# Moving the sums of weights to one engine, and earlier starts for raw weights and first-stage steps, in a fused Fourier-mixing and feed-forward kernel

## The chip, the cores and the metric

The kernel runs on one core of one Trainium2 chip. The metric is the device time of one execution in microseconds (us), as the median of several runs. The core has five engines, each of which takes its own instructions in order: TensorE (PE, matrix products into PSUM), VectorE (DVE), ScalarE (ACT), GpSimd (POOL) and SyncE (SP, which here only issues transfers). Transfers between HBM and SBUF are issued from SP, ACT and POOL and run on 16 DMA engines. Semaphores tie the engines together.

## The reference

```python
def _attn_ref(x, filt_r, filt_i):            # x: 8 x 3008 x 256
    X = np.fft.rfft(x, axis=1)
    F = (filt_r + 1j * filt_i)[None, :, :]   # 1505 x 256
    return np.fft.irfft(X * F, n=x.shape[1], axis=1)

def _moe_ref(x, w_in, w_out):                # x: 24064 x 256, w_in: 256 x 2048, w_out: 2048 x 256
    h = x @ w_in
    g = h - np.tanh(h)
    return g @ w_out
```

The second function works on the result of the first. The two weight matrices arrive as 64-bit floats, which the kernel reads as pairs of 32-bit words.

## The kernel before

**Stages.** The length of 3008 is 64 x 47. A sequence is transformed in stages of matrix products: a first stage (`first`, L273; `first0` and `first1` for the first two sequences), a middle (`middle`) that finishes the transform, multiplies by the filter and goes back half of the way, and a last stage (`last`, L526) that gives a group of 4 x 128 positions in transposed form. Between the stages the data goes through HBM (`ct1`, `ct2`). The feed-forward part then runs on each group.

**Units.** One group has four units, U = 4i + u, and a unit is one quarter u of the hidden width. In loop step U of the main loop (L1284) TensorE makes the first product of unit U (`up`, L565, or `up_plain`, L637, for U under 4), ScalarE and VectorE the activation of unit U - 1 (`shrink`, L678), and TensorE the second product of unit U - 2 (`down`, L729, or `down_plain`). `up` and `down` use seven products where eight would be needed, on sums of the weights: `wu` and `wd` have seven slots each, of which four are loaded and three (slots 4, 5 and 2) are sums; slot 6 is overwritten as well. `up_plain` and `down_plain` use the four loaded slots alone, so group 0 can run before the sums are there. The sums of quarter u of `wu` are `sums(u)`, those of `wd` are `sums(4 + u)`: one addition and three subtractions of 128x256 (L220 to L228). The activations need their own combinations for the seven products: `combine` (L557), of 128x512 for `t` and of 128x256 for `tu`, on GpSimd once all weights are ready.

**Raw weights.** `converted` (L165) loads 128x512 raw values (512 KB) and makes 32-bit floats of them: one ScalarE instruction (L175), then five or six of VectorE (L177 to L195). `weights` (L237) is a generator over 16 such jobs, of which jobs 5 to 15 run beside the start of the main loop, on buffers lent by the middle stage (`ft`, `a2`, `xy`), loaded from GpSimd's queue. After certain jobs it goes on with sums (`after`, L1208).

**The order.** All instructions stand in the order in which the Python program emits them; there is no scheduler. Inside a unit `up` calls back: `d` and `e` advance the second product, `s` the activation, `t(k)`, k = 0 to 4, everything else. `converting(n)` (L1310) takes n instructions from the generator `late` (the weights, and from U = 6 on a list of sums): two in each `t`, three in each of four `e`. `t(k)` at position 20c + 5u + k of a sequence (c is the group in it) also takes one step of one other stage: `last` at (u, k) = (3, 2), otherwise a step of the first stage of sequences 1 and 2 when the next entry of `due` (L1278) has come, in units 0 to 3 at any k and later only at k = 2.

**A first-stage step** here is `x_sb` and `f` loaded two steps ahead from SP, eight matmuls (L295) into the two PSUM banks with the tags t and y, two ScalarE copies (L297) into the single buffer `a1`, and a write to HBM from ScalarE's queue (L300). `last` uses the banks t and y too (`pu`, L537; copies at L541, L544, L545); `up` accumulates in banks x, y and z, each held once, and VectorE empties them at L601 (y), L618 and L634 (z) and L626 (x).

**Before the loop.** Sequence 0 goes through all stages first. Its last transfers are e2, the reload of `ct2` for the first `last` (`rest`, L1034). GpSimd then copies one column of e2 to `there_yet` (L1203), so that its next instructions, the raw loads of jobs 7 and 8 (L169), wait for e2. TensorE runs products that nobody reads (`warmer`, L999) until the first `pu`.

Of the kernel before, what the change touches and what calls it, by code (L numbers as in the profile page):

```python
# [9 lines left out]
F32 = mybir.dt.float32  # L10
# [17 lines left out]
NX = NH // XH  # L28
# [10 lines left out]
LEAD = 34  # L39
# [72 lines left out]
def kernel(  # L112
# [10 lines left out]
    V, G, ACT = nc.vector, nc.gpsimd, nc.scalar  # L123
# [14 lines left out]
    cst = ctx.enter_context(tc.tile_pool(name="cst", bufs=1))  # L138
# [81 lines left out]
    def sums(u):  # L220

        w = (wu if u < 4 else wd)[:, :, 256 * (u % 4):256 * (u % 4) + 256]
        by = G if 4 <= u < 7 else V
        by.tensor_add(w[:, 4], w[:, 6], w[:, 3])
        yield
        for to, one_in, less in ((5, 4, 0), (2, 1, 5), (6, 0, 6)):
            by.tensor_sub(w[:, to], w[:, one_in], w[:, less])
            yield  # L228

    def begun(tiles, job, queue=nc.sync):  # L230
# [6 lines left out]
    def weights(tiles, jobs, queue, began, ahead, after=()):  # L237

        began += [begun(tiles, job, queue) for job in jobs[len(began):ahead]]
        yield  # L240
        for k in range(len(jobs)):
            pending[0] = len(jobs) - k
            for n, _ in enumerate(began[k]):
                yield
                if after and n == 2 and k + 1 < len(jobs):
                    next(began[k + 1])
            if k + ahead < len(jobs):
                began.append(begun(tiles, jobs[k + ahead], queue))
            pending[0] = len(jobs) - k - 1
            for u in dict(after).get(k, ()):  # L250
                yield from sums(u)
# [272 lines left out]
    e2s, uts = {}, {}  # L524
# [38 lines left out]
    hs, gs = {}, {}  # L563

    def up(U, d, e, s, t):  # L565

        i, u = divmod(U, 4)
# [32 lines left out]
        shrinks(0)  # L600
        V.tensor_add(h[:, 0, :, 0:w], Y, s1)  # L601
        e()
        shrinks(1)
        if not close:
# [7 lines left out]
        d()  # L612
        shrinks(3)
        e()
        t(2)
        mm(X, 7, False)
# [333 lines left out]
    with tc.tile_pool(name="tr", bufs=2) as tr, tc.manual_schedule():  # L950
# [16 lines left out]
        with tc.tile_pool(name="pro", bufs=1) as pro, \  # L967
# [66 lines left out]
            def rest(a, n, queues):  # L1034

                e2 = e2s[0][0]
                for j in range(4):
                    queues[j % len(queues)].dma_start(
                        e2[NA * j + a:NA * j + a + n],
                        dram(ct2[0], (NA * j + a) * NH * DM, [[NH * DM, n], [1, CH * DM]]))  # L1040
# [128 lines left out]
            for g in range(last_g + 1):  # L1169
# [27 lines left out]
                if g == 2:  # L1197
# [1 line left out]
            rest(0, SG * (last_g - 1), [nc.sync])  # L1199
            way_back()  # L1200
            rest(SG * (last_g - 1), NA - SG * (last_g - 1), [nc.sync])
            there_yet = cst.tile([128, 1], F32, name="there_yet")
            G.tensor_copy(there_yet, e2s[0][0][:, 0, 0:1])  # L1203
            fs = first(2, z2, [(1, c) for c in range(2, NX)])
            next(fs)
            convert(100)
            late = weights(tiles1, jobs[5:], G, ahead, 3,
                           after={6: (0,), 8: (1,), 10: (2, 3, 4, 5, 6)})  # L1208
            next(late)
            for _ in ones_1:  # L1210
                pass
# [2 lines left out]
        with tc.tile_pool(name="dn", bufs=2) as dn, \  # L1214
# [60 lines left out]
                                 start=True, stop=True)  # L1275
            for _ in range(4):
                next(late)
            due = [7 + (LEAD - 7) * k / (NX + 4) for k in range(NX + 4)]  # L1278
            plan = []
            kinds = {(2, 0): "there", (1, 3): "back"}  # L1280
            kinds.update({at: "filter" for at in FILTERED})
# [2 lines left out]
            for U in range(total + 2):  # L1284
                i, u = divmod(U, 4)
                if U == 6:
                    assert not pending
                    late = sums(7)
                if U == 3:
                    G.dma_start(mats[:, 0:10 * PAD], wide_d[0:KM])  # L1290
                if U < total:
# [18 lines left out]
                def converting(n):  # L1310

                    for _ in range(n):
                        if next(late, pending) is pending:
                            pending.clear()
# [5 lines left out]
                def e():  # L1320

                    next(dw, None)
                    converting(3 if U > 1 else 1)

                def s():

# [85 lines left out]
```

## Time and profile before

| | us |
|---|---|
| median of 3 runs | 2584.98 |
| lowest and highest run | 2583.92, 2587.75 |
| the profiled execution | 2587.2 |
| its span, first to last instruction | 2585.3 |
| TensorE busy | 2556.4 |
| VectorE busy | 1821.1 |
| ScalarE busy | 1661.8 |
| GpSimd busy | 1475.9 |

The profile comes from one execution; its span is 1.9 us shorter than its time. A line of the view by order of time has the start in us from the span's start, the time taken, engine, line, operation, out<-in, shapes, the number of instructions merged, and in brackets the idle time of the engine just before and what ended it ("issue": nothing that the profile shows). A transfer's line is its issue and not its landing. PE rows are matmuls; PEld, the weight load, overlaps them.

### The profile page before, as it was taken

Reading aid. Unit: us, or ns where it says so; the run is one execution under the profiler, and the core shown is the slowest. Engines: PE = TensorE matmul, PEld = TensorE weight load, DVE = VectorE, ACT = ScalarE, POOL = GpSimd, SP = SyncE. Lnnn points to the kernel's source line nnn. Section 1 sums busy time; section 2 is a strip of 40 time slices with the busy share of each in tenths; the row PEclk is TensorE's granted clock in tenths of the full one; section 3 lists DMA queues with packets and bytes.
Section 4 is the critical chain, followed back from the end, with each engine's and each line's share of the span. In section 5 each row is a group of like instructions: output and inputs, shape, how many; then the busy total and the mean of one; then the engine's idle time right before and its main releaser. Section 6 shows DMA issues by size and latency. Waiting matters only on the chain.

```text
span 2585.3 us, 43442 instructions
## 1 busy us (share of the span) xinstructions
PE 2556.4 (99%) x16596; PEld 2176.2 (84%) x16596; DVE 1821.1 (70%) x2222; ACT 1661.8 (64%) x2482; POOL 1475.9 (57%) x1138
## 2 busy tenths in 40 slices
PE   8999999999999999999999999999999999999998
PEld 7668888888898888988888888888889888898887
DVE  6877776877567775778657876588766877555555
ACT  4556666666666666666666666666666666666665
POOL 5366665666556665665646565466655766545552
PEclk9999999999999999999999999999999999999999
DMA  8863216441434324333243432444231322110110
GB/s 222 265 178 105 70 30 123 111 102 44 95 75 106 86 59 93 84 88 94 50 101 80 102 78 51 94 96 103 66 71 42 93 66 43 33 32 18 25 21 18
DMA packets 345333, 214.30 MB, mean 83 GB/s; under 512 B 245337, under 2 KB 316535, under 8 KB 341469
## 3 DMA queue, kind: packets, MB, share of 16 engines
q1 hardware_dynamic: 321551, 170.82, 28.7%
q10 hardware_dynamic: 12142, 23.60, 3.0%
q0 software_dynamic: 11424, 17.03, 2.4%
q8 instruction: 132, 2.16, 0.3%
q14 instruction: 84, 0.69, 0.1%
HBM read 130.72 MB, written 83.39 MB: 83 GB/s over the span
## 4 chain that ended last, share of the span: by engine, by line
PE 96%; DVE 1%; DMA 1%; issue 0%; ACT 0%; POOL 0%; ACTq 0%; DVEq 0%; POOLq 0%
PE o L748 43%; PE x L578 25%; PE z L578 12%; PE y L578 6%; PE pm L360 2%; PE pu L537 2%; PE pf L307 1%; PE o L803 1%; PE pf L295 1%; PE o L648 0%; DMA fh<-f 0%; PE pm L362 0%; DMA neg<-in_filt_i_dram 0%; DMA mats_sb<-mats 0%; PE x L648 0%
## 5 line engine op out<-in xcount | busy, mean ns | idle before, releaser
L748 PE MATMUL o<-t,wd 128*128 128x256 f32 (+1 forms) x3008 | 762.1, 376 | 0.0
L558 POOL TENSOR_TENSOR t<-h 128x512 f32<-128x512 f32 (+1 forms) x186 | 305.3, 1641 | 740.1 <-DVE h L700 718.7
L700 DVE TENSOR_TENSOR h<-h,y 128x1024 f32<-128x1024 f32 (+1 forms) x384 | 577.3, 1503 | 165.4 <-ACT y L696 161.8
L748 PEld LDWEIGHTS o<-t,wd 128*128 128x128 f32 x3008 | 569.2, 190 | 82.4 <-POOL o L776 15.1
L578 PE MATMUL x<-tu,wu 128*128 128x256 f32 (+1 forms) x2256 | 579.0, 379 | 0.0
L748 PE MATMUL o<-h,wd 128*128 128x256 f32 (+1 forms) x2256 | 572.8, 376 | 1.8 <-DVE h L700 1.8
L584 ACT COPY s<-x 128x512 f32<-128x512 f32 (+1 forms) x188 | 108.8, 579 | 601.3 <-PE x L578 556.5
L748 PEld LDWEIGHTS o<-h,wd 128*128 128x128 f32 x2256 | 426.0, 190 | 71.4 <-issue 20.5
L578 PEld LDWEIGHTS x<-tu,wu 128*128 128x128 f32 x2256 | 420.9, 190 | 66.8 <-issue 13.5
L693 ACT ACTIVATE y<-y 128x1024 f32<-128x1024 f32 (+1 forms) x384 | 399.3, 1040 | 12.1
L696 ACT ACTIVATE y<-y 128x1024 f32<-128x1024 f32 (+1 forms) x384 | 399.8, 1041 | 4.6
L690 ACT ACTIVATE y<-h 128x1024 f32<-128x1024 f32 (+1 forms) x384 | 400.3, 1042 | 3.5 <-DVE h L626 1.7
L559 POOL TENSOR_TENSOR t<-h,t 128x512 f32<-128x512 f32 (+1 forms) x186 | 306.2, 1646 | 14.6
L560 POOL TENSOR_TENSOR t<-h 128x512 f32<-128x512 f32 (+1 forms) x186 | 288.4, 1551 | 0.0
L561 POOL TENSOR_TENSOR t<-h,t 128x512 f32<-128x512 f32 (+1 forms) x186 | 287.4, 1545 | 0.0
L584 ACT COPY u<-x 128x512 f32<-128x512 f32 (+1 forms) x376 | 213.7, 568 | 56.6 <-PE x L578 53.9
L626 DVE COPY h<-x 128x512 f32<-128x512 f32 (+1 forms) x188 | 127.9, 680 | 136.7 <-PE x L578 136.4
L578 PE MATMUL z<-ut,wu 128*128 128x256 f32 (+1 forms) x752 | 191.1, 377 | 3.6 <-DVE h L618 3.6
L578 PE MATMUL x<-ut,wu 128*128 128x256 f32 (+1 forms) x752 | 190.7, 376 | 0.0
L578 PE MATMUL y<-ut,wu 128*128 128x256 f32 (+1 forms) x752 | 190.0, 375 | 0.0
L578 PE MATMUL z<-tu,wu 128*128 128x256 f32 (+1 forms) x752 | 190.0, 375 | 0.0
L601 DVE TENSOR_TENSOR h<-y,s 128x512 f32<-128x512 f32 (+1 forms) x188 | 126.6, 673 | 69.6 <-PE y L578 62.3
(197 smaller groups left out, 2758.0 us busy)
## 6 DMA issues: line engine op xcount, KB each, us to landing
ft<-filt SPq DMA_DIRECT2D x28, 1024.0 KB
ct<-nn SPq DMA_DIRECT2D x56, 512.0 KB
e<-ct SPq DMA_DIRECT2D x47, 512.0 KB
a<-ct SPq DMA_DIRECT2D x112, 192.0 KB
out_dram<-ot SPq DMA_DIRECT2D x1248, 16.0 KB
x_sb<-in_x_dram SPq DMA_DIRECT2D x74, 256.0 KB
ct<-a ACTq DMA_DIRECT2D x62, 256.0 KB
gt<-g_pairs SPq DMA_DIRECT2D x42, 128.0 KB
```

What stands on the lines that cost most here:

```text
L558: by.tensor_sub(t[0], b[0][1], b[0][0])
L559: by.tensor_sub(t[1], b[1][1], t[0])
L560: by.tensor_sub(t[2], b[1][1], b[0][1])
L561: by.tensor_sub(t[3], b[1][0], t[1])
L578: nc.tensor.matmul(bank[:, k], wu[:, q - 1, (2 * u + k) * 128:(2 * u + k + 1) * 128], rhs[q - 1], start=(first and k == 0), stop=True, ski ...
L584: ACT.copy(t, X)
L626: V.tensor_copy(h[:, 2, :, 0:w], X)
L690: ACT.activation(y[k], ht[k], AF.Arctan, scale=TURN)
L693: ACT.activation(y[k], y[k], AF.Tanh, scale=BEND)
L696: ACT.activation(y[k], y[k], AF.Square, scale=SCALE, accum_out=y_sums[:, 2 * U + k // 2:2 * U + k // 2 + 1])
L700: V.tensor_mul(ht[k], ht[k], y[k])
L748: nc.tensor.matmul(product(q), wd[:, q - 1, (2 * u + k) * 128: (2 * u + k + 1) * 128], rhs[q - 1][:, k], start=(u == 0 and k == 0 and q == ...
```

## The change

Three things. All sums are made on VectorE; those of three quarters of `wd` were on GpSimd. Of the sums that followed the last raw weights (wu's quarters 2 and 3, wd's 0, 1 and 2), only wu's quarter 2 and wd's quarter 0 stay there; wu's quarter 3 and wd's 1, 2 and 3 are spread over units 6 and 7, two instructions in each `t` and none in `e`. The copy to `there_yet` is gone, so the raw loads behind it wait only for their own buffers. The dues of the first-stage steps of sequences 1 and 2 start at position 4 and not 7, with the same end.

```diff
     def sums(u):
         w = (wu if u < 4 else wd)[:, :, 256 * (u % 4):256 * (u % 4) + 256]
-        by = G if 4 <= u < 7 else V
-        by.tensor_add(w[:, 4], w[:, 6], w[:, 3])
+        V.tensor_add(w[:, 4], w[:, 6], w[:, 3])
         yield
         for to, one_in, less in ((5, 4, 0), (2, 1, 5), (6, 0, 6)):
-            by.tensor_sub(w[:, to], w[:, one_in], w[:, less])
+            V.tensor_sub(w[:, to], w[:, one_in], w[:, less])
             yield
...
-            there_yet = cst.tile([128, 1], F32, name="there_yet")
-            G.tensor_copy(there_yet, e2s[0][0][:, 0, 0:1])
...
             late = weights(tiles1, jobs[5:], G, ahead, 3,
-                           after={6: (0,), 8: (1,), 10: (2, 3, 4, 5, 6)})
+                           after={6: (0,), 8: (1,), 10: (2, 4)})
...
-            due = [7 + (LEAD - 7) * k / (NX + 4) for k in range(NX + 4)]
+            due = [4 + (LEAD - 4) * k / (NX + 4) for k in range(NX + 4)]
...
                 if U == 6:
                     assert not pending
-                    late = sums(7)
+                    late = (None for u in (3, 5, 6, 7) for _ in sums(u))
...
                     next(dw, None)
-                    converting(3 if U > 1 else 1)
+                    converting((U < 6) * (3 if U > 1 else 1))
```

LEAD is 34 and NX is 6, so there are ten steps.

## The prediction

> **What bounds the kernel now.** I read the page first, then the windows by stage, then the order of time of TensorE, VectorE, GpSimd and ScalarE where TensorE is not full. From the page:
>
> ```profile
> span 2585.3 us, 43442 instructions
> ...
> PE 2556.4 (99%) x16596; PEld 2176.2 (84%) x16596; DVE 1821.1 (70%) x2222; ACT 1661.8 (64%) x2482; POOL 1475.9 (57%) x1138
> ...
> PE 96%; DVE 1%; DMA 1%; issue 0%; ACT 0%; POOL 0%; ACTq 0%; DVEq 0%; POOLq 0%
> ```
>
> TensorE is busy 99% of the span, and the chain of work is 96% TensorE. Matmuls are neither added nor removed, so the change can only move TensorE's idle time (2585.3 - 2556.4 = 28.9 us) and the time in which its clock is held down. The windows say where both lie (columns: stretch, its length, then busy us of PE, PEld, DVE, ACT, POOL, granted clock, DMA share, GB/s):
>
> ```profile
> 128.00:136.00 8.00, 5.88 (x15) 3.71 (x15) 6.23 (x15) 3.51 (x7) 4.09 (x6) 0.79 0.85 224
> 136.00:156.00 20.00, 15.04 (x53) 9.97 (x52) 19.66 (x25) 8.51 (x14) 18.98 (x23) 0.98 0.76 213
> ```
>
> From 128 to 156 us TensorE stands for 7.1 us. That is units 3 and 4 (a unit is one quarter of the hidden width of one group), where the sums of weights are made. In the second stretch VectorE and GpSimd are both full. TensorE in order of time:
>
> ```profile
> 120.54 1.89 PE L295 MATMUL pf<-x_sb,f 128*128 128x256 f32 x8
> ...
> 130.35 3.00 PE L295 MATMUL pf<-x_sb,f 128*128 128x256 f32 x8 [2.12 <-issue]
> 133.14 2.37 PE L648 MATMUL o<-ut,wu 128*128 128x448 f32 x4
> 135.34 1.67 PE L803 MATMUL o<-h,wd 128*128 128x448 f32 x4
> 136.85 1.03 PE L578 MATMUL x<-ut,wu 128*128 128x256 f32 x4
> ...
> 145.73 1.13 PE L295 MATMUL pf<-x_sb,f 128*128 128x256 f32 x4 [1.40 <-DVE h L601]
> ...
> 155.16 2.08 PE L578 MATMUL z<-ut,wu 128*128 128x256 f32 x4 [3.57 <-DVE h L618]
> 157.03 1.73 PE L578 MATMUL x<-ut,wu 128*128 128x256 f32 x4
> ```
>
> Three waits: A 2.12, B 1.40, C 3.57 us. After A and C the next matmuls are slow: 3.00 against 1.89 and 2.37 against 1.67 (together 1.8 us), then 2.08 and 1.73 against 1.03 (1.75 us). After B only 0.1 is lost. With that A costs 3.9, B 1.5, C 5.3: 10.7 us.
>
> The Trainium skill, "TensorE: Matmul & The Clock Gate", section "What's actually happening", has the clock fall after about 3.4 us without work. Here 2.12 us was enough (clock 0.79 in the first window), so the row decides.
>
> **The change part by part.**
>
> *1. The step behind the `pu` matmuls (wait A).* First-stage matmuls write the PSUM banks t and y. The step at 130.35 stands next but one behind `pu`, which fills the same banks, and VectorE empties them only here:
>
> ```profile
> 129.57 0.68 DVE L545 TENSOR_TENSOR ut<-pu,odd 128x512 f32<-128x512 f32 x1
> ```
>
> It ends at 130.25, and the step starts. The new dues put steps at positions 4, 7, 10, 13, 16, 19 instead of 7, 10, 13, 16, 18, so the built order has one more step at the end of unit 0 and this one two products later, at the end of unit 3. The extra step (1.7 us) is taken out of unit 9, which nets to nothing. Between `pu` and the moved step now lie three products of 1.5 us; the banks are free in time and A's 3.9 us goes. What is late next: the step now stands right before unit 4, whose second product writes bank y. ScalarE must copy the step out first, and its one buffer a1 is free only when the previous step's write has landed:
>
> ```profile
> 125.28 0.33 ACTq L300 DMA_DIRECT2D ct<-a  x1
> ...
> 133.88 1.07 ACT L297 COPY a<-pf 128x512 f32<-128x512 f32 x2 [4.01 <-DMA ct<-a]
> ```
>
> That is 8.6 us from issue to copy. The previous step's copies stand about 1 us later in the new order (one step more ahead of them), so these end near 133.88 + 1.07 + 1.1 = 136.1. Unit 4 begins at 136.85 - 3.9 + 1.7 = 134.65, and y is wanted one product of 0.86 later, at 135.5. Price 0.6; bounds 0 (a write shorter by 0.6) and 4 (longer by 1.6, with the clock's 1.8).
>
> *2. The sums leave GpSimd (waits B and C).* Sums 4, 5, 6 were twelve instructions on GpSimd, of which these rows are the first and the last:
>
> ```profile
> 138.17 0.74 POOL L224 TENSOR_TENSOR wd<-wd 128x256 f32<-128x256 f32 x1
> ...
> 151.68 0.96 POOL L227 TENSOR_TENSOR wd<-wd 128x256 f32<-128x256 f32 x1 [0.57 <-PE o L803]
> ```
>
> VectorE alone (the first four rows) and beside them:
>
> ```profile
> 122.24 0.69 DVE L188 SCALAR_TENSOR_TENSOR xy<-a,xy 128x512 f32<-128x512 uint32 x1
> 122.97 0.76 DVE L195 TENSOR_TENSOR wd<-xy 128x256 f32<-128x256 f32 x2
> ...
> 125.75 1.08 DVE L700 TENSOR_TENSOR h<-h,y 128x896 f32<-128x896 f32 x1
> ...
> 132.09 0.42 DVE L224 TENSOR_TENSOR wu<-wu 128x256 f32<-128x256 f32 x1
> ...
> 138.31 0.89 DVE L186 TENSOR_SCALAR xy<-xy 128x512 int32<-128x512 int32 x1
> ...
> 140.37 2.97 DVE L195 TENSOR_TENSOR wd<-xy 128x256 f32<-128x256 f32 x2
> ...
> 147.17 1.62 DVE L188 SCALAR_TENSOR_TENSOR xy<-a,xy 128x512 f32<-128x512 uint32 x1
> 148.83 1.70 DVE L195 TENSOR_TENSOR wd<-xy 128x256 f32<-128x256 f32 x2
> 150.45 1.61 DVE L700 TENSOR_TENSOR h<-h,y 128x896 f32<-128x896 f32 x1
> 151.98 0.94 DVE L224 TENSOR_TENSOR wu<-wu 128x256 f32<-128x256 f32 x1
> ```
>
> The last five lose 2.21, 0.93, 0.94, 0.53 and 0.52 against the rows above them, 5.1 us; five smaller ones, of which the 0.89 is the first, bring it to 7.3. VectorE's order up to unit 6 hardly changes: where the four sums of wu's last quarter stood (behind L224 at 151.98) stand the four of wd's first. So L618, which ends C, comes up to 7.3 us earlier. TensorE wants it earlier too: by the 5.0 us of B and C, and by A less part 1's price, 3.9 - 0.6 = 3.3. 8.3 against 7.3 leaves 1.0, and L626 behind three sums (0.42 each) holds the next x for some 0.6. Price 1.6; bounds 0 and 3.8 (only the five quoted rows recovered). A gap below 1.4 costs no clock. Parts 1 and 2 save 10.7 - 0.6 - 1.6 = 8.5.
>
> *3. Sixteen sums in units 6 and 7.* Before, four stood there; now sums 3, 5, 6, 7 do: twelve more, 0.42 each. They stand in groups of two. The four of sums 5 fall into unit 6, where VectorE waits for others (1.17 before its L618, in the first of these rows):
>
> ```profile
> 183.46 0.69 DVE L618 TENSOR_TENSOR h<-z,u 128x512 f32<-128x512 f32 x1 [1.17 <-ACT u L584]
> ...
> 195.57 0.69 DVE L544 TENSOR_TENSOR ut<-pu,odd 128x512 f32<-128x512 f32 x1 [0.80 <-ACT odd L541]
> ...
> 196.78 0.68 DVE L618 TENSOR_TENSOR h<-z,u 128x512 f32<-128x512 f32 x1
> ```
>
> Sums 6 and 7 fall into unit 7, ahead of its L618, while GpSimd combines t and later tu:
>
> ```profile
> 171.27 1.27 POOL L558 TENSOR_TENSOR t<-h 128x512 f32<-128x512 f32 x1 [13.08 <-DVE h L700]
> ...
> 187.07 2.19 POOL L558 TENSOR_TENSOR t<-h 128x512 f32<-128x512 f32 x1 [6.56 <-DVE h L700]
> ...
> 193.65 2.25 POOL L561 TENSOR_TENSOR t<-h,t 128x512 f32<-128x512 f32 x1
> ```
>
> ```profile
> 199.19 1.03 PE L578 MATMUL z<-ut,wu 128*128 128x256 f32 x4
> ```
>
> L618 ends at 197.46 and TensorE wants it at 199.19: 1.7 us of slack, with 0.8 idle ahead of L544 it is 2.5. Eight sums cost 3.4 alone; beside GpSimd 0.85 each (half of the pair at 148.83), 6.8. So 0.9 to 4.3 us of wait; I take 2.0, nearer the low end, because GpSimd's four instructions end at 195.9 whatever stands beside them, and half of the sums come later. An upper bound is among the rivals.
>
> *4. Raw weights no longer wait for e2.* Before, GpSimd stood until e2's reload was in:
>
> ```profile
> 82.39 0.18 POOL L1203 COPY there_yet<-e 128x1 f32<-128x1 f32 x1 [12.74 <-DMA f<-f_both]
> 82.93 0.74 POOL L169 DMA_DIRECT2D a<-in_moe_w_out_dram  x1 [0.37 <-issue]
> ```
>
> ```profile
> 83.51 1.27 PE L537 MATMUL pu<-gt,e 64*64 64x64 f32 x64
> ```
>
> Now two loads of 512 KB start up to the 12.7 us earlier for which that instruction kept GpSimd waiting, beside e2's last write and reload. VectorE can't use them sooner: its first instruction on them stands behind L544 of the first `pu`. So there is no gain here but 1 MB less traffic right after, where the extra step's 1.3 MB comes in. The loss: e2 has 1.1 us of slack (82.39 to 83.51, covered by the warming matmuls). What queued loads do to such a write, with raw loads in flight and without:
>
> ```profile
> ct<-e POOLq DMA_DIRECT2D x2, 240.0 KB, 6.6
> ...
> ct<-e POOLq DMA_DIRECT2D x4, 240.0 KB, 3.1
> ```
>
> Bounds: nothing, and 3.5 on the write and 3.5 on the reload less 1.1, 5.9. Those two stood in GpSimd's own queue behind the raw loads; e2's go by SyncE and ScalarE. I take 1.0.
>
> **Sum.** 8.5 - 2.0 - 1.0 = 5.5 us off 2585.3 of span, so 2581.7 for that execution (2587.2). The median of the runs is 2585.0; from it, 2579.5.
>
> **Rivals.**
> *R1, all hidden.* Sums fit between PSUM copies and e2 keeps its slack: 2585.0 - 8.5 = 2576.5. For it: VectorE's waits of 1.17 and 0.80; against it: the 1.7 us at L618. The Trainium skill, "DMA: Bandwidth & Descriptors", section "Queues, rings and completion order", says that each DMA engine alternates between queues packet by packet, which would keep e2 from standing behind the raw loads; no row here shows raw loads in one queue slowing another.
> *R2, part of it is eaten.* Unit 7 waits over 2 us and pays the clock (2.0 + 1.8 more), or the write chain of a1 takes its bound (3 more): 2582 to 2584.
> *R3, slower: VectorE becomes the bound in unit 7.* If a sum beside GpSimd must wait for a whole instruction of it, the pair at 140.37 is the price (2.97 / 2 = 1.49 each): 8 x 1.49 - 2.5 + 1.8 = 11.2, so 2585.0 - 8.5 + 1.0 + 11.2 = 2588.7; at 2.19 each (t's row) 2594. It decides from about 1.2 us a sum. Against it: t's four instructions can hold VectorE only while they run. The Trainium skill, "SBUF - State Buffer", section "Who interferes with whom", has the port that the two engines share locked for a whole instruction, the loser blocked; L195's 2.97 agrees, but t's 2.19 against its 1.27 at 171.27 shows that the loss falls on both.
> *R4, nothing.* B and C are VectorE's own backlog and return behind wd's first sums: about 2585. Against it: the slow rows lie exactly where GpSimd adds.
>
> **How the numbers follow.** A measurement tells 0.2% (5.2 us) from no change. Forecast 0.45 (2576.8 to 2582), R1 0.15, R2 0.22, R3 0.12, R4 0.06. Faster by over 0.2% is below 2579.8: of the forecast's own 0.45 some 0.30, R1's 0.15, and 0.03 of cases with still less waiting, 0.48. Slower by over 0.2% is above 2590.2: R3's upper half and e2 at its bound, 0.10. The rest, 0.42. Range 2574.3 to 2588.7: from R1 with parts 1 and 2 free of their price (2585.0 - 10.7) to R3's lower price.
>
> **What would show it.** Part 1: no wait of L295 behind `pu`, y of unit 4 behind ScalarE's L297. Part 2: L195 at 0.76 a pair in unit 4, wait C under 1 us. Part 3: waits for L618 or L626 around unit 7. Part 4: `pu` later than 83.5. A `pu` later by over 3 us, or a wait over 6 us in unit 7, makes the forecast wrong; so does a TensorE clock that stays down after a short gap.

## The result and the profile after

| | before | after |
|---|---|---|
| median, us (12 runs each, taken together) | 2588.08 | 2582.41 |
| lowest and highest run, us | 2583.92, 2591.72 | 2580.93, 2585.17 |
| ratio of after to before, with its 95% interval | | 0.9979 [0.9971, 0.9986] |
| the profiled execution, us | 2587.2 | 2582.09 |
| its span, us | 2585.3 | 2580.2 |

The change saves 0.21%, 5.4 to 5.7 us. The prediction said 5.5 us; its 2579.5 stands below the 2582.4 measured because the three runs that it started from had a median 3.1 us below that of the twelve. All ratios here are of runs in the fast state; three of e9's seven runs (3816 to 6900 us) are in the slow one, so that its ratio rests on four.

In the changed kernel lines 224 to 1201 of before have numbers lower by one and those behind 1203 lower by three: L294 is the first-stage product `pf`, L296 its copy into `a1`, L536 `pu`, L577 `up`, L600, L617, L625 and L633 VectorE's emptying of y, z, x and z. The page of the kernel after:

```profile
span 2580.2 us, 43441 instructions
...
PE 2554.9 (99%) x16596; PEld 2174.5 (84%) x16596; DVE 1817.4 (70%) x2234; ACT 1662.0 (64%) x2482; POOL 1466.7 (57%) x1125
```

TensorE has as many matmuls as before. VectorE has 12 instructions more and is busy for 3.7 us less, although work came over to it from GpSimd. The same stretches as in the prediction, and that of unit 7, after:

```profile
128.00:136.00 8.00, 8.00 (x85) 4.74 (x85) 5.99 (x13) 5.08 (x9) 5.80 (x7) 1.00 0.97 258
136.00:156.00 20.00, 18.05 (x69) 12.74 (x69) 17.58 (x35) 12.47 (x19) 15.28 (x17) 1.00 0.98 257
...
180.00:200.00 20.00, 18.33 (x141) 15.21 (x140) 19.93 (x23) 10.16 (x15) 12.49 (x9) 1.00 0.08 13
```

Units 3 and 4 gain 5.1 us of busy TensorE and the clock stays at 1.00 (0.79 and 0.98 before). Unit 7 gives 1.7 us of it back (TensorE was busy for all 20.00 us there before), and VectorE is now busy there for 19.93 of 20 us (15.95 before). TensorE in order of time, after:

```profile
134.74 1.89 PE L294 MATMUL pf<-x_sb,f 128*128 128x256 f32 x8
...
139.45 1.13 PE L577 MATMUL y<-ut,wu 128*128 128x256 f32 x4 [1.95 <-ACT a L296]
...
151.61 1.03 PE L577 MATMUL z<-ut,wu 128*128 128x256 f32 x4
152.47 1.03 PE L577 MATMUL x<-ut,wu 128*128 128x256 f32 x4
153.33 1.03 PE L577 MATMUL y<-ut,wu 128*128 128x256 f32 x4
...
182.28 1.03 PE L577 MATMUL y<-ut,wu 128*128 128x256 f32 x4
...
186.33 1.13 PE L577 MATMUL z<-tu,wu 128*128 128x256 f32 x4 [0.44 <-DVE h L633]
...
190.29 1.15 PE L536 MATMUL pu<-gt,e 64*64 64x64 f32 x60 [0.84 <-DVE h L600]
...
196.35 1.13 PE L577 MATMUL z<-ut,wu 128*128 128x256 f32 x4 [0.39 <-DVE h L617]
...
198.18 1.03 PE L577 MATMUL y<-ut,wu 128*128 128x256 f32 x4
```

A, B and C are gone. In their place stands one wait of 1.95 us, for ScalarE's copy of the moved step, with no slow matmuls behind it. The first product into y marks where a unit begins. The marks of before, for units 5, 7 and 8:

```profile
158.60 1.03 PE L578 MATMUL y<-ut,wu 128*128 128x256 f32 x4
...
187.55 1.03 PE L578 MATMUL y<-ut,wu 128*128 128x256 f32 x4
...
200.92 1.03 PE L578 MATMUL y<-ut,wu 128*128 128x256 f32 x4
```

Unit 5 begins 5.27 us earlier (153.33 against 158.60), although by then one first-stage step more is done (1.73 us) and the run was already 1.23 us late at the first product of the stage ahead of the first `pu`, before and after:

```profile
72.82 1.08 PE L420 MATMUL pe<-xy,mats_sb 96*96 96x128 f32 x8 [0.55 <-DVE xy L400]
```

```profile
74.05 1.08 PE L419 MATMUL pe<-xy,mats_sb 96*96 96x128 f32 x8 [1.31 <-DVE xy L399]
```

These 1.23 us do not look like the change's: 0.42 are there before the first raw load that it moves (at 69.90), and 0.76 are the longer wait in this row (1.31 against 0.55), which e13 below has too (1.24) though it keeps `there_yet`, and which the five other kernels without it don't have (0.55).

So from that product to unit 5, with as many steps done, it is 158.60 - 72.82 = 85.78 us before and 153.33 - 74.05 - 1.73 = 77.55 after: **8.2 us saved**, with the first `pu`'s wait of 0.67 for e2 in after's share (part 4 below). Unit 7 then takes 198.18 - 182.28 = 15.90 us against 13.37: **2.5 us lost**. With the 1.23 us that leaves 4.5 of the 5.1 us between the two spans; the last 0.6 lie in the rest of the kernel and have no place of their own. VectorE, after:

```profile
144.91 0.69 DVE L188 SCALAR_TENSOR_TENSOR xy<-a,xy 128x512 f32<-128x512 uint32 x1
145.63 0.76 DVE L195 TENSOR_TENSOR wd<-xy 128x256 f32<-128x256 f32 x2
146.31 1.08 DVE L699 TENSOR_TENSOR h<-h,y 128x896 f32<-128x896 f32 x1
147.31 0.41 DVE L223 TENSOR_TENSOR wu<-wu 128x256 f32<-128x256 f32 x1
...
181.63 1.22 DVE L449 TENSOR_TENSOR nn<-xy,ft 128x1024 f32<-128x1024 f32 x1
182.76 1.50 DVE L223 TENSOR_TENSOR wd<-wd 128x256 f32<-128x256 f32 x1
184.29 1.38 DVE L226 TENSOR_TENSOR wd<-wd 128x256 f32<-128x256 f32 x1
185.60 0.68 DVE L633 TENSOR_TENSOR h<-z,u 128x512 f32<-128x512 f32 x1
...
187.81 1.82 DVE L226 TENSOR_TENSOR wd<-wd 128x256 f32<-128x256 f32 x2
...
191.29 0.41 DVE L223 TENSOR_TENSOR wd<-wd 128x256 f32<-128x256 f32 x1
191.74 0.43 DVE L226 TENSOR_TENSOR wd<-wd 128x256 f32<-128x256 f32 x1
...
194.41 1.28 DVE L226 TENSOR_TENSOR wd<-wd 128x256 f32<-128x256 f32 x2
```

Without sums on GpSimd the five slow rows of before are back at their time alone: L195's pairs 0.76 (2.97 and 1.70 before), L188 0.69 (1.62), L699 1.08 (1.61) and L223 0.41 (0.94). In unit 7 the eight sums take 1.50 + 1.38 + 1.82 + 0.41 + 0.43 + 1.28 = 6.82 us, against 3.4 alone. The long ones stand beside GpSimd's `t` and `tu`, of which these are the first two and the last of `t` and the first of `tu`:

```profile
181.80 2.18 POOL L557 TENSOR_TENSOR t<-h 128x512 f32<-128x512 f32 x1 [6.50 <-DVE h L699]
184.05 1.34 POOL L558 TENSOR_TENSOR t<-h,t 128x512 f32<-128x512 f32 x1
...
186.77 2.25 POOL L560 TENSOR_TENSOR t<-h,t 128x512 f32<-128x512 f32 x1
194.58 0.84 POOL L557 TENSOR_TENSOR tu<-ut 128x256 f32<-128x256 f32 x1 [5.56 <-DVE ut L544]
```

### The profile page after: what moved, and what is told of

The parts are those of the page before. It is cut to its first block, busy times and chain, and to the rows that moved or that the text cites. A ratio compares the mean times of both kernels' runs of the same rounds, so it can differ in the third digit from the quotient of the medians.

```text
span 2580.2 us, 43441 instructions
## 1 busy us (share of the span) xinstructions
PE 2554.9 (99%) x16596; PEld 2174.5 (84%) x16596; DVE 1817.4 (70%) x2234; ACT 1662.0 (64%) x2482; POOL 1466.7 (57%) x1125
## 4 chain that ended last, share of the span: by engine, by line
PE 94%; DMA 2%; DVE 2%; issue 0%; ACT 0%; POOL 0%; SPq 0%; ACTq 0%; DVEq 0%; POOLq 0%
PE o L747 43%; PE x L577 25%; PE z L577 12%; PE y L577 6%; PE pm L359 2%; PE pu L536 2%; PE pf L306 1%; DMA x<-in_x_dram 1%; DMA filt<-in_filt_r_dram 1%; PE o L802 0%; DMA a<-in_moe_w_out_dram 0%; PE pm L361 0%; PE pf L294 0%; DMA ct<-e 0%; DVE h L699 0%
## 5 line engine op out<-in xcount | busy, mean ns | idle before, releaser
L699 DVE TENSOR_TENSOR h<-h,y 128x1024 f32<-128x1024 f32 (+1 forms) x384 | 573.5, 1494 | 166.3 <-ACT y L695 162.9
L577 PE MATMUL x<-tu,wu 128*128 128x256 f32 (+1 forms) x2256 | 578.9, 379 | 0.0
L577 PEld LDWEIGHTS x<-tu,wu 128*128 128x128 f32 x2256 | 420.9, 190 | 66.8 <-issue 13.3
L625 DVE COPY h<-x 128x512 f32<-128x512 f32 (+1 forms) x188 | 127.9, 680 | 135.0 <-PE x L577 134.7
L577 PE MATMUL y<-ut,wu 128*128 128x256 f32 (+1 forms) x752 | 190.1, 375 | 2.0 <-ACT a L296 2.0
L577 PE MATMUL z<-tu,wu 128*128 128x256 f32 (+1 forms) x752 | 190.1, 375 | 0.4 <-DVE h L633 0.4
L577 PE MATMUL z<-ut,wu 128*128 128x256 f32 (+1 forms) x752 | 190.1, 375 | 0.4 <-DVE h L617 0.4
L577 PE MATMUL x<-ut,wu 128*128 128x256 f32 (+1 forms) x752 | 190.0, 375 | 0.0
L600 DVE TENSOR_TENSOR h<-y,s 128x512 f32<-128x512 f32 (+1 forms) x188 | 126.6, 673 | 69.1 <-PE y L577 62.5
```

The lines of the kernel that those rows point to most:

```text
L577: nc.tensor.matmul(bank[:, k], wu[:, q - 1, (2 * u + k) * 128:(2 * u + k + 1) * 128], rhs[q - 1], start=(first and k == 0), stop=True, ski ...
L625: V.tensor_copy(h[:, 2, :, 0:w], X)
L699: V.tensor_mul(ht[k], ht[k], y[k])
```

## The experiments

**Theory**: the gain is VectorE's. With GpSimd's sums gone it runs at its full rate in unit 4, and its work there sets when unit 5 begins; dues and `there_yet` are worth little. **Rival**: the gain is made of separate waits, so that the dues bring what part 1 credits them with (3.3 us), and each further wait of TensorE taken away brings its length.

All kernels in one table. "To unit 5" is the time from the first product of the stage ahead of the first `pu` (L420 before, L419 after) to the first product into y of unit 5, made comparable as above, by 1.73 us for each first-stage step more or less than before's. "Unit 7" is y to y.

| kernel | sums 4 to 6 on | ratio to before [95%] | to unit 5, us | unit 7, us |
|---|---|---|---|---|
| before | GpSimd | 1 | 85.78 | 13.37 |
| after | VectorE | 0.9979 [0.9971, 0.9986] | 77.55 | 15.90 |
| e1 | VectorE | 0.9975 [0.9965, 0.9984] | 78.17 | 13.37 |
| e2 | GpSimd | 1.0008 [0.9999, 1.0017] | 89.20 | 13.38 |
| e3 | GpSimd | 1.0003 [0.9994, 1.0012] | 87.10 | 13.37 |
| e4 | VectorE | 0.9979 [0.9969, 0.9988] | 76.92 | 15.91 |
| e5 | VectorE | 0.9979 [0.9970, 0.9989] | 77.93 | 15.91 |
| e6 | VectorE | 0.9968 [0.9956, 0.9980] | 79.23 | 13.37 |
| e7 | VectorE | 0.9985 [0.9976, 0.9994] | 79.92 | 15.92 |
| e8 | VectorE, GpSimd busy | 0.9998 [0.9989, 1.0007] | 84.99 | 15.92 |
| e9 | VectorE | 0.9964 [0.9950, 0.9978] | 80.13 | 13.38 |
| e10 | VectorE | 0.9968 [0.9956, 0.9980] | 78.53 | 13.37 |
| e12 | VectorE | 0.9973 [0.9963, 0.9984] | 80.47 | 15.36 |
| e13 | VectorE | 0.9983 [0.9975, 0.9992] | 78.94 | 15.37 |

"To unit 5" falls into two sets: 76.9 to 80.5 wherever VectorE works alone, 85.0 to 89.2 wherever GpSimd works beside it, whatever dues and `there_yet` are (e8's 85.0 is not GpSimd's work alone, see there). Each "to unit 5" is of one profiled execution, though (in e2, e8 and e12 the slowest of its kernel, in e3 the second slowest), and holds other waits too: the first `pu`'s for e2's reload in every kernel without `there_yet` (0.7 us in after, 1.2 in e7, 1.5 in e6, 2.0 in e2, 2.2 in e8, 2.5 in e12; none in the eight that keep it), 3.2 for `x_sb` in e3, and the slow clock (1.8 us in e9). VectorE's own stretch leaves these out: from the start of its first copy of unit 3's `pu` (L544 in before) to the end of unit 4's L626 it takes 25.4 to 27.9 us in before, e2 and e3, 22.7 in e8 and 17.3 to 20.3 in all others.

### One part of the change at a time

**e1_dve_in_place**: before, with the sums on VectorE and all places kept.

```diff
-        by = G if 4 <= u < 7 else V
+        by = V
```

> The kernel before, with the twelve sums of GpSimd given to VectorE at the places where they stand; nothing else is changed. Theory (GpSimd's adds slow VectorE beside them): the pair L195 in unit 4 takes 0.76 us and not 1.7 to 3.0, the waits for L601 (1.40) and L618 (3.57) with their slow matmuls go, 6.8 us, and the twelve sums behind L618 cost 0 to 2; wait A (2.1 us behind pu) stays. Ratio to the kernel before 0.9975 to 0.9980. Rival (VectorE's own amount of work makes the waits): twelve more instructions on a full engine, waits B and C stay or grow by up to 5 us, ratio 1.000 to 1.002.

Measured 0.9975 [0.9965, 0.9984]: this one line brings as much as the whole change. TensorE of e1 around wait A:

```profile
133.77 1.96 PE L295 MATMUL pf<-x_sb,f 128*128 128x256 f32 x8 [2.18 <-issue]
```

Wait A stands as before (2.18 against 2.12), only without slow matmuls behind it; the waits for L601 and L618 are gone.

**e2_no_gate**: before, without `there_yet`.

```diff
-            there_yet = cst.tile([128, 1], F32, name="there_yet")
-            G.tensor_copy(there_yet, e2s[0][0][:, 0, 0:1])
```

> The kernel before without the copy to there_yet. Theory (two raw loads beside e2's write and reload delay the first pu by about half a us and bring nothing): pu at 84 to 85.5 instead of 83.5, ratio 1.0000 to 1.0006. Rival (raw weights that are there earlier let VectorE run ahead): waits B and C shrink, ratio under 0.9993.

Measured 1.0008 [0.9999, 1.0017], at the edge of a loss and slightly above what was expected. The first `pu` of e2 waits for e2's reload, as part 4 of the prediction has it:

```profile
86.74 1.54 PE L537 MATMUL pu<-gt,e 64*64 64x64 f32 x64 [1.96 <-DMA e<-ct]
```

It stands past the 84 to 85.5 expected; 1.4 us of that is the run's lateness at the first product of the stage ahead (74.20 against 72.82).

**e3_due4**: before, with the dues from 4.

```diff
-            due = [7 + (LEAD - 7) * k / (NX + 4) for k in range(NX + 4)]
+            due = [4 + (LEAD - 4) * k / (NX + 4) for k in range(NX + 4)]
```

> The kernel before with the dues from position 4. Theory (the waits are a chain: VectorE sets the pace in unit 4): wait A goes (3.9 us) and 1 to 2 us for bank y come in its place, but L618 still ends near 155 to 156 us, so wait C grows by what A gives; what is left is the extra step done early, 1.7 us, ratio 0.9990 to 0.9996. Rival (the waits add up independently): 2 to 4 us saved, ratio 0.9985 to 0.9992 with wait C still about 3.6.

Measured 1.0003 [0.9994, 1.0012]: no gain, where both expectations had one. A and C are gone, and TensorE of e3 waits for VectorE in unit 4 instead, longer than A and B together, and pays the clock (2.08 against 1.13). Ahead of that, in unit 2, its third first-stage step waits for a load:

```profile
109.47 1.97 PE L295 MATMUL pf<-x_sb,f 128*128 128x256 f32 x8 [3.15 <-DMA x_sb<-in_x_dram]
...
153.23 2.08 PE L295 MATMUL pf<-x_sb,f 128*128 128x256 f32 x4 [3.95 <-DVE h L601]
```

e5 below, with the same dues, has no such wait. So this trace can't say what the dues alone are worth with the sums on GpSimd; the ratio's interval leaves at most 0.0006, 1.6 us.

**e4_spread_only**: the sums as after, dues and `there_yet` as before.

```diff
-        by = G if 4 <= u < 7 else V
+        by = V
...
-                           after={6: (0,), 8: (1,), 10: (2, 3, 4, 5, 6)})
+                           after={6: (0,), 8: (1,), 10: (2, 4)})
...
-                    late = sums(7)
+                    late = (None for u in (3, 5, 6, 7) for _ in sums(u))
...
-                    converting(3 if U > 1 else 1)
+                    converting((U < 6) * (3 if U > 1 else 1))
```

> The kernel before with all that concerns the sums (all on VectorE, spread over units 6 and 7), the dues and the copy to there_yet as before. Theory: waits B and C go (6.8 us), unit 7 loses 2 to 3, wait A stays: ratio 0.9980 to 0.9987. Rival (the gain of the whole change is the first-stage step's): ratio 0.9995 to 1.0005.

Measured 0.9979 [0.9969, 0.9988], the ratio of the whole change. Wait A is still there in e4 (2.06 us, the matmuls behind it 1.97), and unit 7 has lost its 2.5 us.

**e5_gate_kept**: after, with `there_yet` put back.

```diff
+            there_yet = cst.tile([128, 1], F32, name="there_yet")
+            G.tensor_copy(there_yet, e2s[0][0][:, 0, 0:1])
             fs = first(2, z2, [(1, c) for c in range(2, NX)])
```

> The changed kernel with the copy to there_yet put back. Theory (the early dues need the traffic of the two raw loads out of the way): as with the dues alone, the third first-stage step waits about 3 us for its x_sb near 107 us, while the first pu is about 0.6 us earlier: 1.5 to 3 us slower than the change, ratio to the kernel before 0.9985 to 0.9992. Rival (removing the copy only costs): 0.5 to 1 us faster than the change, ratio 0.9974 to 0.9978.

Measured 0.9979 [0.9970, 0.9989]: the theory's number fell. What `there_yet` is worth is not clear of noise in any ratio (e2's is the nearest to it); in the traces it moves waits about. The first `pu` doesn't wait and y of unit 4 waits only 0.69 (1.95 after), but the x behind unit 4 now waits 0.60 for L625, and unit 5 begins at 153.98 (153.33 after).

### What sets the beginning of unit 5

**e8_gpsimd_dummies**: after, with sixteen additions of 128x192 on a buffer of GpSimd's own at the places where it made sums. They change no value and nobody waits for them.

```diff
+    busy = cst.tile([128, 192], F32, name="busy")
+    G.memset(busy, 0.0)
...
             for u in dict(after).get(k, ()):
                 yield from sums(u)
+            if k == 10 and after:
+                for _ in range(16):
+                    G.tensor_add(busy, busy, busy)
+                    yield
```

> The changed kernel with sixteen additions of 128x192 on GpSimd, on a tile that nobody else uses, at the places where its sums stood before (work added, no data depends on it). Theory (GpSimd's SBUF reads slow VectorE's instructions with two SBUF inputs): L195 at 1.7 to 3 us a pair in unit 4, VectorE 5 to 7 us late, waits for L600 and L617 of 3 to 6 us with or without slow matmuls after them, ratio 0.9995 to 1.0010. Rival (the dependence on GpSimd's results, or the place of the sums, made the waits): no wait, ratio 0.9979.

Measured 0.9998 [0.9989, 1.0007]: in the ratio the gain is gone. VectorE of e8 is slow again (0.94 a pair against 0.76, 1.39 against 1.08; L705 is L699 of after), but not as slow as expected (1.7 to 3 a pair), and TensorE's waits for L606 and L623 (L600 and L617 of after) are 0.56 and 2.39, at the low edge of the 3 to 6 us expected:

```profile
151.32 0.94 DVE L195 TENSOR_TENSOR wd<-xy 128x256 f32<-128x256 f32 x2
152.19 1.39 DVE L705 TENSOR_TENSOR h<-h,y 128x896 f32<-128x896 f32 x1
```

```profile
157.15 1.65 PE L583 MATMUL z<-ut,wu 128*128 128x256 f32 x4 [2.39 <-DVE h L623]
```

That GpSimd reads and writes SBUF beside VectorE is enough to slow it; the data need not depend on each other. But e8's whole loss is not the dummies'. Its first dummy is at 144.74, and ahead of that TensorE waits 2.19 us at the first `pu` for e2's reload (0.67 after) and at unit 3's `pu` for a copy of ScalarE's that after doesn't wait for:

```profile
132.52 0.33 PE L542 MATMUL pu<-gt,e 64*64 64x64 f32 x4 [1.46 <-ACT a L302]
```

Of the 7.4 us between e8 and after in "to unit 5", 3.6 are there before VectorE's first copy of that `pu`; another 3.6 are VectorE's stretch (22.7 us against 19.1), which is the dummies' work in the main, and less than half of what GpSimd's sums cost in before (27.9). The trace is of the slowest of e8's eleven runs, which lie between 2583.2 and 2591.8; how the 4.9 us between the two ratios divide is not known. The sixteen also take sixteen turns of `late`, so a little of the loss may be order and not contention.

**e7_no_step19**: after, without the first-stage step behind `pu` at position 19, so that y of unit 4 has nothing to wait for; the step is made up for in unit 9.

```diff
-                    elif due and due[0] <= pos and (U < 4 or u < 3 and k == 2):
+                    elif due and due[0] <= pos and (pos < 19 or u < 3 and k == 2):
```

> The changed kernel without the first-stage step at position 19 (it goes to unit 4, and each later step one place back). Theory (y of unit 4 waits for ScalarE's copies of that step out of bank y): the wait of 1.95 us goes; ScalarE still stands for the last raw load until about 137.7, which can hold the copy s and so x by up to 1 us: 1 to 2 us saved, ratio 0.9971 to 0.9975. Rival (the raw load holds TensorE whatever stands there): the same wait at another matmul, ratio 0.9979.

Measured 0.9985 [0.9976, 0.9994]: the theory of that run fell; the rival's ratio held, but not its reason, the raw load. The wait of y (1.95) is gone and a longer one stands in its place, for VectorE. TensorE and VectorE of e7:

```profile
145.26 1.13 PE L294 MATMUL pf<-x_sb,f 128*128 128x256 f32 x4 [2.38 <-DVE h L600]
```

```profile
144.18 0.43 DVE L180 TENSOR_SCALAR xy<-xy 128x512 int32<-128x512 int32 x1
144.52 0.68 DVE L600 TENSOR_TENSOR h<-y,s 128x512 f32<-128x512 f32 x1
```

L600 starts right behind L180, without idle time: VectorE's own queue holds it, not y, which TensorE finished at 137.1. Unit 5 begins at 154.06, no earlier than after, with a step less done.

**e10_no_step18**: the same question without the change's dues, on e9 (below), against it.

```diff
-                    elif due and due[0] <= pos and (U < 4 or u < 3 and k == 2):
+                    elif due and due[0] <= pos and (pos < 18 or u < 3 and k == 2):
```

> The same with the first-stage step behind pu at the end of unit 3 left out there (it is made up for in unit 9), so that wait A cannot stand. Theory (VectorE's backlog in unit 4 sets when unit 5 begins, so an idle TensorE before it costs nothing): the wait comes back for L601, L618 or L626 in unit 4, ratio within 0.0006 of the run with the step. Rival (wait A is a cost of its own, 2.1 us): 0.0008 less than the run with the step, 0.9958 to 0.9963, and no new wait in unit 4.

Measured 0.9968 [0.9956, 0.9980] against e9's 0.9964 [0.9950, 0.9978], as the theory has it. Wait A is gone, and TensorE of e10 stands as long in unit 4:

```profile
141.22 1.13 PE L295 MATMUL pf<-x_sb,f 128*128 128x256 f32 x4 [1.89 <-DVE h L601]
...
147.33 1.13 PE L578 MATMUL z<-ut,wu 128*128 128x256 f32 x4 [0.24 <-DVE h L618]
...
149.05 1.13 PE L578 MATMUL x<-ut,wu 128*128 128x256 f32 x4 [0.60 <-DVE h L626]
```

2.73 us in place of 2.18. With the sums on VectorE, TensorE's waits in units 3 and 4 are in the main one wait, for VectorE, that can be taken early or late.

**e13_vector_lighter**: e10 with sums 1 put behind the last raw quarter and six sums from unit 5 on, so that VectorE should have less ahead of L601.

```diff
-                           after={6: (0,), 8: (1,), 10: (2, 4)})
+                           after={6: (0,), 10: (1,)})
...
-                    late = (None for u in (3, 5, 6, 7) for _ in sums(u))
+                    late = (None for u in (2, 4, 3, 5, 6, 7) for _ in sums(u))
```

> The kernel before with all sums on VectorE, no first-stage step behind pu at the end of unit 3, sums 1 moved behind the last raw quarter and six sums spread from unit 5 on: VectorE has 1.65 us less ahead of unit 4's L601 and 3.4 us less ahead of its L618. If VectorE's backlog is what holds unit 4, taking both the step and these sums away brings 1.5 to 2.5 us over the run with the step alone left out: ratio 0.9956 to 0.9963. If that backlog is not what holds it, no more than 0.4 us: 0.9966 to 0.9970.

Measured 0.9983 [0.9975, 0.9992], outside both expectations, because the edit didn't do what it was meant to. `converting` counts instructions: taking four sums away ahead of L601 pulls four instructions of the next raw job into their turns, and those are longer. From L545's start to L601's start VectorE ran 11.4 us in e13, and 10.1 in e10 (130.41 to 140.48). VectorE of e13:

```profile
132.14 0.68 DVE L545 TENSOR_TENSOR ut<-pu,odd 128x512 f32<-128x512 f32 x1
...
143.51 0.68 DVE L601 TENSOR_TENSOR h<-y,s 128x512 f32<-128x512 f32 x1
```

With 1.3 us more on VectorE ahead of L601, TensorE waits 2.35 us for it (1.89 in e10), and "to unit 5" is 0.4 us longer than e10's, though VectorE then reaches the end of L626 earlier (17.8 us from its first L544, 19.2 in e10) and the waits of z and x are gone. 2.0 of the 3.9 us between the two ratios are lost in unit 7 (15.37 us), where the list ends as in e12 below. The wait for L601 fits a bound by VectorE, but a VectorE with less to do ahead of L601, which was to show it, was never run: whether taking work off VectorE ahead of L601 brings unit 5 forward stays open.

### Where the sums go

**e6_sums_unit5**: after, with the sixteen sums begun one unit earlier, so that none is left in unit 7.

```diff
-                if U == 6:
+                if U == 5:
                     assert not pending
...
-                    converting((U < 6) * (3 if U > 1 else 1))
+                    converting((U < 5) * (3 if U > 1 else 1))
```

> The changed kernel with the sixteen spread sums begun in unit 5 instead of unit 6, so that all but six lie before unit 6 and none beside GpSimd's combine in unit 7. Theory (VectorE waits beside GpSimd's combine, and TensorE for it, in unit 7): the waits of 0.44, 0.84 and 0.39 us for L633, L600 and L617 go, unit 7 takes 13.4 us from y to y and not 15.9, 2.5 us saved, ratio 0.9966 to 0.9972. Rival (VectorE's wait for PE in unit 5 is no real slack, the loss moves there): ratio as the change, 0.9979.

Measured 0.9968 [0.9956, 0.9980]. Unit 7 of e6 is back at 13.37 us (y at 183.15 and 196.52), without a wait. The trace shows the 2.5 us; the ratios' intervals still overlap with after's 0.9979 [0.9971, 0.9986].

**e9_sums_only_unit5**: e4 with the edits of e6, so nothing but the sums is changed.

> The kernel before with nothing but the sums changed: all on VectorE, sums 3, 5, 6, 7 spread from unit 5 on; dues from 7 and there_yet stay. Theory (the sums are the whole gain, dues and there_yet are worth nothing): as with all parts and the sums from unit 5, ratio 0.9966 to 0.9972, unit 7 takes 13.4 us from y to y, wait A stays at about 2.1 us with matmuls at 1.9 to 2.0 behind it. Rival (dues and there_yet bring what the prediction's part 1 says, 2 to 3 us): 0.9977 to 0.9982.

Measured 0.9964 [0.9950, 0.9978]: not to be told from e6, though dues and `there_yet` are as before. One expectation missed: A's 2.18 us are followed by slow matmuls here. TensorE of e9:

```profile
132.66 3.65 PE L295 MATMUL pf<-x_sb,f 128*128 128x256 f32 x8 [2.18 <-issue]
```

**e12_six_from_unit5**: e6 with sums 2 and 4 put off as well.

```diff
-                           after={6: (0,), 8: (1,), 10: (2, 4)})
+                           after={6: (0,), 8: (1,), 10: ()})
...
-                    late = (None for u in (3, 5, 6, 7) for _ in sums(u))
+                    late = (None for u in (2, 4, 3, 5, 6, 7) for _ in sums(u))
```

> The kernel after with sums 2 and 4 also moved, so that six sums (2, 4, 3, 5, 6, 7) are spread from unit 5 on, two instructions at a step, and none stands behind sums 1 in unit 4. Theory: the waits of z (0.24) and x (0.60) in unit 4 go, that of y (0.67) stays, and unit 5 and 6 take the eight instructions in VectorE's idle time: 0.8 us less than with four sums from unit 5, ratio 0.9962 to 0.9969. Rival (what is put off returns in units 5 and 6 beside GpSimd's t): waits of 1 us or more there, 0.9972 or above.

Measured 0.9973 [0.9963, 0.9984]: the rival's number, in unit 7 and not in 5 or 6. The list now ends in unit 7, with two instructions of sums 6 and all of sums 7. VectorE of e12:

```profile
185.76 2.91 DVE L226 TENSOR_TENSOR wd<-wd 128x256 f32<-128x256 f32 x2
...
190.81 1.49 DVE L223 TENSOR_TENSOR wd<-wd 128x256 f32<-128x256 f32 x1
```

Three of these sums beside `t` take 4.4 us, and unit 7 takes 15.36 us: nearly as much as with eight sums. It is the sums that meet `t` which cost.

## Why the prediction came out right, step by step

**The sum of parts 1 and 2 was right, its split was not.** Predicted: 8.5 us, of which 3.3 from the dues (A's 3.9 less 0.6) and 5.2 from the sums. Measured: 8.2 in after's trace, 8.9 with the 0.67 of part 4 taken out. But the sums alone bring 7.6 (e1) and 8.9 (e4) with wait A standing; the dues add nothing to them that the ratios show (after and e4, both 0.9979; e6 0.9968 and e9 0.9964), though intervals of 0.001 either way, 2.6 us, would not show a small part. The term that was mis-sized is *"the banks are free in time and A's 3.9 us goes"*: A goes, but with the sums on VectorE it is not a cost of its own. VectorE is full from `pu` to the end of unit 4, TensorE has to wait for it once, and A is one place for that. (In after VectorE is last but for some 0.7 us: its L625 ends at 151.64, and TensorE comes to the next x at 152.47.) Two wrong sizes thus made a right sum. Part of that is luck; part is that the price of 1.6 had bounded both together by VectorE's 7.3 us. And with 1.23 us that are not the change's and 0.6 without a place, an agreement to a few tenths is closer than the account itself.

**The price of 0.6 at y of unit 4** was 1.95. The order and the place were right (no wait of L294 behind `pu`, y behind ScalarE's L296). Not the write of `a1` decided, but a load: in after's order of time of ScalarE a raw job's first instruction stands ahead of the copy, waits for its data, and the copy follows without idle time.

```profile
137.77 0.67 ACT L175 ACTIVATE xy<-a 128x512 f32<-128x512 f32 x1 [4.29 <-DMA a<-in_moe_w_out_dram]
138.34 1.06 ACT L296 COPY a<-pf 128x512 f32<-128x512 f32 x2
```

**The price of 1.6 at the end of unit 4** was 0 in after, where z (151.61) and x (152.47) don't wait. Both prices together were 2.2 and measured 1.95. They are one quantity too: with y's wait at 0.69 in e5 and 0.67 in e6, x waits 0.60, behind three sums as the prediction has it (in e6 z waits 0.24 as well).

**VectorE's loss** came back as computed (all of the five rows' 5.1 us), e1 shows that it goes with GpSimd's sums, and e8 that other additions on GpSimd bring part of it back. The Trainium skill, "SBUF — State Buffer", section "Who interferes with whom", says that a VectorE instruction with two SBUF inputs contends with a GpSimd instruction that reads SBUF, and one with at most one SBUF input, outside VectorE's 2-port modes, does not. After's rows agree: beside `t` the sums take 1.50 and 1.38 (0.42 alone), while L633, one of whose inputs is in PSUM, takes 0.68 there as elsewhere. The ends of these rows fit turns of whole instructions: the first sum ends 0.28 us behind `t`'s first instruction (184.26 and 183.98), the second 0.28 us behind its second (185.67 and 185.39; the same pairs in e6 and e12 end 0.28 to 0.29 us behind), and `t`'s first is itself long (2.18, and 1.27 in the prediction's row at 171.27) where it starts inside VectorE's L449, which has two inputs in SBUF and ends at 182.85. So that both engines lose, which R3 has as a sign against whole turns, is none: each waits for the other.

**Part 3** said 6.8 us for the eight sums of unit 7 (measured 6.82) and 2.0 us of wait (measured 2.5, of which 0.44 + 0.84 + 0.39 stand in brackets; unit 6 loses nothing). The place was right in part: the prediction has the wait at L618, L617 after, where only the 0.39 stands. R3's price of 1.49 a sum, a wait for a whole instruction of GpSimd's, is that of the first two (1.50, 1.38), not of all eight: the next two beside `t` paid 0.91 each, two beside `tu` 0.64 and two alone 0.42. The gaps stayed under 1 us, and the clock at 1.00.

**Part 4** said 1.0. The first `pu` of after waits 0.67:

```profile
85.30 1.43 PE L536 MATMUL pu<-gt,e 64*64 64x64 f32 x64 [0.67 <-DMA e<-ct]
```

The two raw loads do start early, behind GpSimd's last write of that stage and without a wait; the first of them:

```profile
69.90 0.74 POOL L169 DMA_DIRECT2D a<-in_moe_w_out_dram  x1
```

In the other kernels without `there_yet` the same wait was 1.17 to 2.49, within the bounds given, and in the eight that keep it there was none. So raw loads issued early from GpSimd's queue do delay e2's reload, which SyncE issues, or the write ahead of it; the prediction had left that open. Whether the end sees it is not known: after and e5 have the same ratio, e2 loses 0.0008, 2 us, at the edge of its noise. The row of `there_yet` before names the load of `f`; that GpSimd waited for e2 is the program's text, not the row's.

**The rivals.** R4, that B and C would come back behind wd's first sums, fell with e1. R1 needed a free unit 7: e6 and e9 have it, at 0.9968 and 0.9964. R1's 8.5 us would be 0.9967. R2's 2582 to 2584 holds the median of after, but only because the twelve runs of before lie higher than the three: its saving was 1 to 3 us, and neither of its reasons came, the clock in unit 7 or the write of `a1`.

## What to carry to other kernels

When TensorE waits several times in a stretch where another engine is full, don't add up the waits: work out when the full engine reaches a fixed point behind them, since a wait taken away in front comes back there. Light instructions on GpSimd can be dear if VectorE is full beside them and both read SBUF; they cost less on VectorE, in a stretch where GpSimd does not compute. And where a generator hands out work by a count of instructions, moving some of it later pulls other work forward into its turns.

## What the hardware showed

**The same wait of TensorE can cost the clock or not.** Waits of 2.06 to 2.39 us in units 3 and 4 were followed by slow matmuls in four kernels (before 2.12, e2 2.20, e8 2.39, e9 2.18) and not in four others (e1 2.18, e4 2.06, e13 2.35, e7 2.38). Of the longer ones there those of 3.57 (before), 3.60 (e2) and 3.95 us (e3) were; none under 2 us was. In unit 2 the 3.15 of e3, for `x_sb`, was not either. The Trainium skill, "TensorE: Matmul & The Clock Gate", section "What's actually happening", has the activity window free-running, so that the moment at which the clock rises depends on where in it the first matmul lands. That the outcome of a gap depends in the same way on where it falls would fit these rows, but no run shows it. The section's window of 3.4 us is longer than the waits of 2.12 to 2.39 that did cost.

**A one-input instruction of VectorE was slow too, beside GpSimd's issue of a transfer.** In e7, L177 took 1.17 us (0.42 elsewhere) while GpSimd issued a transfer (its L1254, at 142.66 for 1.26 us), and ended 0.22 us behind that; VectorE of e7:

```profile
142.97 1.17 DVE L177 TENSOR_SCALAR xy<-xy 128x512 f32<-128x512 f32 x1
```

That is 0.75 us on the engine that sets the pace there. Whether other queues for these transfers would save it was not tried.
